# LSH attention and a convolutional feed-forward on one core: weight decoding, convolution taps and the divide with an operand in PSUM

## The chip, the core and the metric

One core of one Trainium2 chip. The metric is device microseconds of one execution, median of the runs shown.

## The reference

Batch 4, 8 heads, 768 positions, head size 64. Keys and queries are hashed to 6 bits each, and a query sees only the keys of its own bucket:

```python
mask = q_bucket[:, :, :, None] == k_bucket[:, :, None, :]
scores = np.where(mask, scale * np.matmul(q, k.transpose(0, 1, 3, 2)), -1000000000.0)
attn = np.exp(scores - np.max(scores, axis=-1, keepdims=True))
attn = attn / (np.sum(attn, axis=-1, keepdims=True) + 1e-09)
x = np.matmul(attn, v)            # then (4, 768, 512), heads side by side
h = np.maximum(x @ w_in, 0.0)     # 512 x 1024
# conv_out: three taps along the sequence, one weight per column and tap
out = h * (1.0 / (1.0 + np.exp(-conv_out))) @ w_out   # 1024 x 512
```

The weights of the feed-forward arrive as float64 and are read as pairs of 32-bit words.

## The kernel before

The order of every engine's instructions is the order of the code. Four batches follow each other, and each has four pairs of heads and then a feed-forward.

A **pair** takes six steps, `i` = 0 to 5 in the loop at L495. It works on two blocks of query columns (416 and 352), three steps each. A step computes the scores of two chunks of 128 keys on TensorE (L294, L295) and their exponentials on ScalarE (L297), and for the chunks of the step before the values (L305) and the row sums' additions: chunks 1 to 4 on GpSimd (L320), chunk 5 on VectorE (L318). The block's last step in line sums over the partitions on TensorE (L328), and VectorE inverts and divides (L331 to L350); the result is split into a high and a low part (L353, L357). Between them the next pair is prepared: row maxima, twelve times two matmuls and a reduction on VectorE (`peak`, L246, L249), in the places that the table `PEAKS` names; the maxima's way through DRAM into row 96 of the queries (`shift_away`, `shift_back`); and for the pair after that the hash (L174), its bits (L180), the high part `hi` of the load `R` (L188), the low part in `R` itself (L192), and the copies into the tiles of Q and K (`place_a`, `place_b`). All those copies and the loads of `R`, `v` and weights go through SP's queue in code order; `bring` (L477) issues at a pair's start the four copies of `place_b`, then the next load of `R`, which must wait until the copies out of `R` have landed, then `v`.

A **feed-forward** has 16 stages (`ffn`, L407): stage `i` computes 128 hidden columns of half the sequence (12 matmuls, L368), ScalarE takes the ReLU and the middle tap, VectorE the two outer taps (L377) and after the sigmoid the product (L381), and GpSimd the low part. `FLAG` = 3 iterations later the stage's output follows (9 matmuls, L392). The hidden banks are a ring of three.

**Weights.** 16 blocks of 128x512 are decoded in batch 0: loaded (`fetch`), |x| on ScalarE (L90), five operations on VectorE (L92 to L100), a cast on ScalarE (L108), two operations on GpSimd (L110, L112). `background` (L132) moves the blocks under way on by some operations at each call. Ten blocks are begun in the pairs of batch 0, six in its feed-forward.

**PSUM** is used as eight banks: a ring S of three times two banks (scores, maxima, sums, outputs) and a ring M of two (values, hash).

## Time and profile before

| | us |
|---|---|
| runs (median) | 809.56, 811.0, 814.94 (811.0) |
| profiled execution | 809.63 |
| its span | 807.8 |

The page gives the busy time of each engine, then the span in 40 slices with the busy share in tenths. [...] In a timeline, a bracket holds the idle time before an instruction and what ended it. "x4" behind a row is a run of four instructions of the same kind.

### The profile page before, as it was taken

What the parts mean: (1) busy time and instruction counts of PE and PEld (TensorE: products, weight loads), DVE (VectorE), ACT (ScalarE), POOL (GpSimd) and SP (SyncE); (2) the same over time, 40 slices, a digit from 0 to 9 for tenths busy, and PEclk for the clock granted to TensorE, in tenths of its full rate; (3) what the DMA queues carried; (4) which work ended last, traced back from release to release, by engine and by line L of the source; (5) the groups of instructions that cost most, each with busy time, mean ns of one, the idle gap of its engine ahead of it and who ended that gap; (6) DMA issues with size and microseconds to landing.
All of it is one profiled execution on the core that took longest, in us unless ns stands there. A gap on an engine that the chain in (4) does not pass through costs nothing.

```text
span 807.8 us, 10032 instructions
## 1 busy us (share of the span) xinstructions
PE 724.2 (90%) x3552; PEld 512.4 (63%) x3552; DVE 562.9 (70%) x758; ACT 361.8 (45%) x582; POOL 404.9 (50%) x264
## 2 busy tenths in 40 slices
PE   6788777786679999999999999999999999999997
PEld 3444443444568855655889755655899755657896
DVE  4479898989895476776766476767766467756664
ACT  4334343435445534444555444444554443445553
POOL 5466666654462374766222365675222466562222
PEclk9797999789789999999999999999999999999999
DMA  4557665625001117646601116655501136500011
GB/s 124 135 179 162 210 174 176 160 47 147 1 0 40 41 24 172 137 113 159 174 4 40 41 37 161 139 148 146 151 0 40 41 69 152 131 3 1 1 40 39
DMA packets 38358, 75.88 MB, mean 94 GB/s; under 512 B 8312, under 2 KB 16774, under 8 KB 38308
## 3 DMA queue, kind: packets, MB, share of 16 engines
q1 hardware_dynamic: 33940, 74.60, 35.1%
q10 hardware_dynamic: 4368, 0.64, 0.5%
q8 instruction: 28, 0.46, 0.2%
q14 instruction: 22, 0.18, 0.1%
HBM read 29.71 MB, written 9.73 MB: 49 GB/s over the span
## 4 chain that ended last, share of the span: by engine, by line
PE 50%; DVE 23%; DMA 15%; issue 5%; ACT 4%; SPq 2%; POOL 1%; ACTq 0%; DVEq 0%
PE o L393 13%; PE v L305 10%; PE spot L368 8%; DMA k<-R 6%; DVE stat L249 5%; PE s L294 5%; DVE ht L377 4%; PE m L246 4%; PE s L295 4%; DMA R<-in_qk 4%; PE h L368 4%; DMA far<-bits 2%; PE sum L328 1%; SPq L207 1%; DVE wuo L92 1%
## 5 line engine op out<-in xcount | busy, mean ns | idle before, releaser
L297 ACT ACTIVATE p<-s 128x836 f32<-128x836 f32 (+1 forms) x192 | 152.8, 810 | 204.9 <-PE s L295 175.9
L249 DVE TENSOR_REDUCE stat<-m 128x1 f32<-128x772 f32 x192 | 181.0, 951 | 80.2 <-PE m L246 79.6
L320 POOL TENSOR_TENSOR ps<-ps,p 128x832 f32<-128x832 f32 (+1 forms) x92 | 161.2, 1752 | 24.2 <-ACT p L297 20.5
L385 POOL TENSOR_TENSOR g<-ht,g 128x384 fp32r<-128x384 f32 x64 | 68.9, 1077 | 207.8 <-ACT g L384 183.7
L305 PE MATMUL v<-p,v 128*64 128x418 f32 (+1 forms) x768 | 155.2, 527 | 13.9 <-DVE bits L180 13.9
L294 PE MATMUL s<-q,k 97*128 97x418 f32 (+1 forms) x384 | 141.1, 368 | 19.5 <-DVE stat L249 9.5
L377 DVE SCALAR_TENSOR_TENSOR ht<-ht,cw 128x384 f32<-128x384 f32 (+1 forms) x128 | 119.1, 931 | 52.3 <-ACT ht L375 49.9
L393 PE MATMUL o<-wo,g 128*128 128x512 f32 x576 | 144.8, 398 | 6.2 <-DVE r L338 6.2
L295 PE MATMUL s<-q,k 128*128 128x418 f32 (+1 forms) x384 | 132.6, 345 | 0.0
L393 PEld LDWEIGHTS o<-wo,g 128*128 128x128 f32 x576 | 108.6, 190 | 28.0 <-DVE r L338 6.6
L246 PE MATMUL m<-k,q 96*128 96x386 f32 x384 | 114.6, 384 | 12.9 <-DVE stat L249 5.9
L320 POOL TENSOR_TENSOR ps<-p,p 128x832 f32<-128x832 f32 (+1 forms) x32 | 60.6, 1893 | 104.9 <-ACT p L297 104.9
L246 PEld LDWEIGHTS m<-k,q 96*128 96x128 f32 x384 | 66.2, 199 | 71.9 <-DVE stat L249 28.6
L294 PEld LDWEIGHTS s<-q,k 97*128 97x128 f32 x384 | 74.2, 193 | 55.3 <-DVE stat L249 20.8
L368 PE MATMUL spot<-xh,wi 128*128 128x386 f32 x320 | 92.5, 351 | 11.7 <-ACT ht L373 11.7
L305 PEld LDWEIGHTS v<-p,v 128*64 128x64 f32 x768 | 48.7, 142 | 77.8 <-issue 60.8
L380 ACT ACTIVATE ht<-ht 128x384 f32<-128x384 f32 x64 | 33.6, 525 | 106.5 <-DVE ht L377 106.5
L295 PEld LDWEIGHTS s<-q,k 128*128 128x128 f32 x384 | 74.7, 194 | 0.7
L368 PEld LDWEIGHTS spot<-xh,wi 128*128 128x128 f32 x320 | 61.0, 194 | 17.3 <-ACT ht L373 13.9
L192 POOL TENSOR_TENSOR R<-R,hi 128x768 fp32r<-128x768 f32 x30 | 59.1, 1971 | 21.6 <-PE hash L174 13.8
L381 DVE TENSOR_TENSOR ht<-ht 128x384 f32<-128x384 f32 x64 | 36.0, 563 | 31.9 <-ACT ht L380 31.9
L368 PE MATMUL spot<-xl,wi 128*128 128x386 f32 x160 | 55.5, 347 | 0.0
(84 smaller groups left out, 735.6 us busy)
## 6 DMA issues: line engine op xcount, KB each, us to landing
R<-in_qk SPq DMA_DIRECT2D x15, 768.0 KB
v<-in_v SPq DMA_DIRECT2D x16, 384.0 KB
k<-hi SPq DMA_DIRECT2D x16, 384.0 KB
q<-hi SPq DMA_DIRECT2D x16, 384.0 KB
out<-osb SPq DMA_DIRECT2D x24, 256.0 KB
q<-R SPq DMA_DIRECT2D x15, 384.0 KB
k<-R SPq DMA_DIRECT2D x15, 384.0 KB
rawi<-in_w_in SPq DMA_DIRECT2D x8, 512.0 KB
```

What stands on the lines that cost most here:

```text
L192: nc.gpsimd.tensor_tensor(R, R.bitcast(F32), self.hi[:, h].bitcast(F32), ALU.subtract)
L246: nc.tensor.matmul(mp[:, half], self.QA[:96, h, t * P:(t + 1) * P], self.K[0][:96, h, half * HS:(half + 1) * HS + 2], start=True, stop=True)
L249: nc.vector.tensor_reduce(self.stat[:, c:c + 1], mp, mybir.AxisListType.XY, ALU.max)
L294: nc.tensor.matmul(sp[:, h], pr.KA[:97, h, ks], pr.Q[0][:97, h, qs], start=True, stop=False)
L295: nc.tensor.matmul(sp[:, h], pr.KB[:, h, ks], pr.Q[1][:, h, qs], start=False, stop=True)
L297: nc.scalar.activation(self.pts[c], sp, AF.Exp, scale=SCALE)
L305: nc.tensor.matmul(self.av[h * D:(h + 1) * D], pr.v[:, c, h, :], self.pts[c][:, h], start=(c == 0), stop=(c == NCK - 1), tile_position=(0, ...
L320: eng.tensor_tensor(self.acc, first if c == 1 else self.acc, pt, ALU.add)
L368: nc.tensor.matmul(hp[:, :HW], w, x[:, c0:c0 + HW], start=(n == 0), stop=(n == 3 * NCC - 1))
L377: nc.vector.scalar_tensor_tensor(t[:, a:z], ht[:, o + k - 1 + a:o + k - 1 + z], cw[:, f, k:k + 1], t[:, a:z], ALU.mult, ALU.add)
L385: nc.gpsimd.tensor_tensor(g[:, 1, :], t, g[:, 0, :].bitcast(F32), ALU.subtract)
L393: nc.tensor.matmul(op, l, r, start=(f == 0 and n == 0), stop=(f == NFC - 1 and n == 2))
```

## The change

Line numbers in the order pieces after the change are those of the changed file: decoding is L106 to L116 there, the reduction of maxima L261, the divide L368, its low part L375, `place_b` L218 and L219, taps L395, product L399.

- Decoding keeps its intermediate in a spare bank of M, so |x| is written to PSUM and each of the five VectorE operations has at most one operand in SBUF. Blocks are begun at steps 2 and 5 of each pair of batch 0 (eight in all) and at iterations 2 to 9 of its feed-forward (eight).
- ReLU works in place in PSUM, and the taps and the product read the hidden stage there. The banks of the hidden ring are the two of S2 (named M2, M3 during a feed-forward) and one of M. The output of a stage follows 4 iterations later in batch 0.
- The divide writes in place in PSUM.
- In batch 0 (`direct`) chunk 5 is not added; `sums` runs over it separately, with two calls more, and 1e-9 is added to the sums.
- `place_b` is in two parts: the copies out of `R` come first, then the load of the next `R` and `v`, then the copies out of `hi`. The hash takes a tile of ring S. The last maximum of a pair moves into the next pair's step 0, `shift_away(4, 2)` from step 0 to 1 and `shift_back(4, 2)` from 1 to 2. Two weight blocks are fetched before the first pair, and two at every third step.

```diff
 FLAG = 3
-RATE = 4
-PEAKS = ((), (1, 2), (0, 1, 2), (0, 1, 2), (1, 2), (1, 2))
-PEAKS_0 = ((0, 1, 2), (0, 1, 2), (0, 1, 2), (0, 1, 2), (1, 2), (1, 2))
+FLAG_0 = 4
+DECODE = 2
+PEAKS = ((2,), (0, 1, 2), (1, 2), (0, 1, 2), (1, 2), (1,))
+PEAKS_0 = ((0, 1, 2), (0, 1, 2), (0, 1, 2), (0, 1, 2), (1, 2), (1,))
...
+    rooms = []
+    def room(name):
+        if rooms:
+            rooms.pop()[0].__exit__(None, None, None)
+        if name:
+            c = tc.tile_pool(name=name, bufs=1, space=PSUM, reuse_waits="tile")
+            rooms.append((c, c.__enter__()))
+    def two_banks(name, k=None):
+        if k is None:
+            k = turns["S"] = (turns.get("S", -1) + 1) % 3
+        pool = rooms[0][1] if k == 2 else ps
+        return pool.tile([P, 2, 512], F32, tag=f"S{k}", name=name, bufs=1)
+    def one_bank(name, k):
+        return (ps if k < 2 else rooms[0][1]).tile([P, 512], F32, tag=f"M{k}", name=name, bufs=1)
...
+    def decode(raw, n, name, bank):
...
+        up, low = (ring(wp, 3, [P, WC], I32, f"w{x}", f"w{x}{name}")[:, :n] for x in "ul")
+        tmp = bank[:, :n]
+        tmpi = tmp.bitcast(I32)
...
-        nc.scalar.activation(lowf, hi, AF.Abs)
-        yield 2
-        V.scalar_tensor_tensor(upf, lowf, F64_MIN, hi, ALU.is_ge, ALU.mult)
-        yield 1
-        V.tensor_scalar(low, up, 3, 0x3FFFFFFF, ALU.logical_shift_left, ALU.bitwise_and)
-        yield 0
-        V.scalar_tensor_tensor(up, up, -0x40000000, low, ALU.bitwise_and, ALU.bitwise_or)
-        yield 2
-        V.tensor_scalar(low, up, -0x800000, None, ALU.bitwise_and)
-        yield 0
-        V.scalar_tensor_tensor(lowf, lo, 2.0 ** -52, lowf, ALU.mult, ALU.mult)
+        nc.scalar.activation(tmp, hi, AF.Abs)
+        yield
+        V.scalar_tensor_tensor(upf, tmp, F64_MIN, hi, ALU.is_ge, ALU.mult)
+        yield
+        V.tensor_scalar(tmpi, up, 3, 0x3FFFFFFF, ALU.logical_shift_left, ALU.bitwise_and)
+        yield
+        V.scalar_tensor_tensor(up, up, -0x40000000, tmpi, ALU.bitwise_and, ALU.bitwise_or)
+        yield
+        V.tensor_scalar(tmpi, up, -0x800000, None, ALU.bitwise_and)
+        yield
+        V.scalar_tensor_tensor(lowf, lo, 2.0 ** -52, tmp, ALU.mult, ALU.mult)
...
+    def split_weight(raw, name, bank):
+        up, low = yield from decode(raw, WC, name, bank)
+        yield
+        yield
         blk = weights[name] = cp.tile([P, 2, WC], F32R, tag=f"w{name}", name=f"w{name}")
         nc.scalar.copy(blk[:, 0, :], up)
-        yield 2
+        yield
         nc.gpsimd.tensor_tensor(up, up, blk[:, 0, :].bitcast(F32), ALU.subtract)
-        yield 1
         nc.gpsimd.tensor_tensor(blk[:, 1, :], up, low, ALU.add)
 
...
+    def spare_bank(name):
+        return one_bank(name, (turns.get("M", 1) + 1) % 2)
+    def decode_next():
+        raw, name = fetched.pop(0)
+        decoding[0] = split_weight(raw, name, spare_bank(f"d{name}"))
+    def decode_on(n=1):
+        for _ in range(n):
+            next(decoding[0], None)
 
...
-            hp = ring(ps, 2, [P, 512], F32, "M", f"hash{self.nm}")
-            turns["M"] -= 1
+            hp = two_banks(f"hash{self.nm}")[:, 0, :]
...
-        def place_b(self):
-            hi, lo = self.hi.bitcast(F32), self.R.bitcast(F32)
-            QB, KB = self.QB.bitcast(F32), self.KB.bitcast(F32)
-            for dst, src in ((QB[:64], hi[:64]), (KB[64:], hi[64:]), (QB[64:], lo[:64]), (KB[:64], lo[64:])):
-                nc.sync.dma_start(dst, src)
+        def place_b(self, low):
+            src = (self.R if low else self.hi).bitcast(F32)
+            QB, KB = (t.bitcast(F32)[64 * k:64 * k + 64] for t, k in ((self.QB, low), (self.KB, 1 - low)))
+            nc.sync.dma_start(KB, src[64:])
+            nc.sync.dma_start(QB, src[:64])
...
+            self.direct = pair.b == 0
...
         def add(self, c):
 
-            if c == 0:
+            if c == 0 or (self.direct and c == NCK - 1):
                 return
             if c == 1:
                 self.acc = ring(wp, EB, [P, 2, WMAX], F32, "e", f"ps{self.nm}")[:, :, :self.w]
-            last = self.j == 1 and self.pair.p == NP - 1
+            last = self.j == 1 and self.pair.p == NP - 1 and not self.direct
             eng = nc.vector if c > DADD - last else nc.gpsimd
...
             self.sm = bank[:, :w]
-            for h in range(2):
-                nc.tensor.matmul(self.sm[h * D:(h + 1) * D], ones, self.acc[:, h],
-                                 start=True, stop=True, tile_position=(0, h * D))
+            parts = [self.acc] + [self.pts[-1][:, :, self.n - w:]] * self.direct
+            for k, part in enumerate(parts):
+                for h in range(2):
+                    nc.tensor.matmul(self.sm[h * D:(h + 1) * D], ones, part[:, h], start=(k == 0),
+                                     stop=(k == len(parts) - 1), tile_position=(0, h * D))
...
             nc.vector.transpose(self.tt[:, 0, :w], self.sm)
-            nc.vector.reciprocal(rec, self.tt[:, 0, :w].rearrange("p (j r) -> p j r", r=32)[:, :, 0])
+            total = self.tt[:, 0, :w].rearrange("p (j r) -> p j r", r=32)[:, :, 0]
+            if self.direct:
+                nc.vector.tensor_scalar(rec, total, 1e-9, None, ALU.add)
+                total = rec
+            nc.vector.reciprocal(rec, total)
             self.rec = rec
...
-            self.xf = self.tt[:, 0, :w]
-            nc.vector.scalar_tensor_tensor(self.xf, self.av[:, self.n - w:], pr.mean, self.tt[:, 1, :w],
-                                           ALU.add, ALU.mult)
+            self.xf = self.av[:, self.n - w:]
+            nc.vector.scalar_tensor_tensor(self.xf, self.xf, pr.mean, self.tt[:, 1, :w], ALU.add, ALU.mult)
...
-        ht = ring(wp, EB, [P, 2, WMAX], F32, "e", f"ht{b}_{half}_{f}").rearrange("p a b -> p (a b)")
-        t = ht[:, 388:388 + HS]
-        nc.scalar.activation(ht[:, :HW], hp[:, :HW], AF.Relu)
+        hp = hp[:, :HW]
+        t = ring(wp, EB, [P, 2, WMAX], F32, "e", f"ht{b}_{half}_{f}")[:, 0, :HS]
         o = 0 if half == 0 else HW - HS
-        nc.scalar.activation(t, ht[:, o:o + HS], AF.Copy, scale=cw[:, f, 1:2])
+        nc.scalar.activation(hp, hp, AF.Relu)
+        nc.scalar.activation(t, hp[:, o:o + HS], AF.Copy, scale=cw[:, f, 1:2])
         for k, a, z in ((0, half == 0, HS), (2, 0, HS - (half == 1))):
-            nc.vector.scalar_tensor_tensor(t[:, a:z], ht[:, o + k - 1 + a:o + k - 1 + z], cw[:, f, k:k + 1],
+            nc.vector.scalar_tensor_tensor(t[:, a:z], hp[:, o + k - 1 + a:o + k - 1 + z], cw[:, f, k:k + 1],
                                            t[:, a:z], ALU.mult, ALU.add)
         yield None
         nc.scalar.activation(t, t, AF.Sigmoid)
-        nc.vector.tensor_tensor(t, ht[:, o:o + HS], t, ALU.mult)
+        nc.vector.tensor_tensor(t, hp[:, o:o + HS], t, ALU.mult)
...
-        s0, m0 = turns["S"], (turns["M"] + 1) % 2
-        spot = ps.tile([P, 2, 512], F32, tag=f"S{(s0 + 1) % 3}", name=f"spot{b}", bufs=1)
+        m0, flag = turns["M"], FLAG if b else FLAG_0
+        room(f"ffn{b}")
 
         def bank(i):
-            k = i % 2 if i < 4 else (i - 1) % 3
-            if k == 0:
-                return ps.tile([P, 512], F32, tag=f"M{m0}", name=f"h{b}_{i}", bufs=1)
-            return spot[:, k - 1, :]
-        for i in range(len(todo) + FLAG):
-            fill(i, ps.tile([P, 2, 512], F32, tag=f"S{s0}", name=f"spare{b}", bufs=1) if i == 2 else None)
+            return one_bank(f"h{b}_{i}", 2 + i % 2 if i < 4 else (2, 3, m0)[(i - 4) % 3])
...
+            decode_on(3)
+            if i >= DECODE and fetched:
+                decode_next()
+                decode_on(3)
...
             if i == len(todo) + 1:
-                turns["S"] = s0
+                room(f"heads{b + 1}")
+                turns["S"] = 1
...
+                half, f = todo[i - flag]
                 if f == 0:
-                    acc[half] = [ps.tile([P, 2, 512], F32, tag=f"S{(s0 + 3 - k) % 3}", name=f"o{b}_{half}_{k}",
-                                         bufs=1) for k in range(2)]
-                output(b, half, f, gs[i - FLAG], acc[half])
+                    acc[half] = [two_banks(f"o{b}_{half}_{k}", 1 - k) for k in range(2)]
...
+            if i >= DECODE:
+                decode_on(3)
...
-    splits.append(decode_taps(cwr))
+    fetch(2)
...
         if n < len(pairs):
-            pairs[n].place_b()
+            pairs[n].place_b(1)
         if n + 1 < len(pairs):
             pairs[n + 1].load()
         if n < len(pairs):
             pairs[n].load_v()
+            pairs[n].place_b(0)
...
-            if i == 1 and n:
+            if i == 2 and n:
                 pr.shift_back(4, 2)
...
-                    if i == 0 and n:
+                    if i == 1 and n:
                         pr.shift_away(4, 2)
...
+                    decode_on()
...
+            if pr.b == 0 and i % 3 == 2:
+                if n == 0 and i == 2:
+                    decoding[0] = decode_taps(cwr, spare_bank("dcw"))
+                    decode_on(6)
+                decode_next()
+            decode_on()
...
-            background(RATE, 1)
+            decode_on()
...
-            if n or i:
-                fetch(1)
-            background(RATE, 1)
+            if i % 3 == 0:
+                fetch(2 if n else 1)
+            decode_on(4 if i == 5 and pr.p == NP - 1 else 1)
```

VectorE, from the end of pair 1 of batch 0 into pair 2, before (`stat` holds row maxima, `wui`, `wli` and `rawi` a block of weights, `ps` row sums):

```order
L249 TENSOR_REDUCE stat_83<-m_2_5_1_739 128x1
L268 STREAM_TRANSPOSE side_2_4_743<-stat_83 128x32
L92 SCALAR_TENSOR_TENSOR wui_1_754<-wli_1_755,rawi_1_466 128x512
L318 SCALAR_TENSOR_TENSOR ps_1_1_683<-ps_1_1_683,p_1_1_5_724 128x2x352
L94 TENSOR_SCALAR wli_1_755<-wui_1_754 128x512
L96 SCALAR_TENSOR_TENSOR wui_1_754<-wui_1_754,wli_1_755 128x512
L249 TENSOR_REDUCE stat_84<-m_3_0_0_813 128x1
```

The same place after it (`di` is the bank of PSUM, `xl` the low part of a pair's result):

```order
L261 TENSOR_REDUCE stat_83<-m_2_5_0_729 128x1
L375 TENSOR_TENSOR xl_1_710<-v_1_0_549,xh_1_709 128x416
L108 SCALAR_TENSOR_TENSOR wui_0_735<-di_0_734,rawi_0_385 128x512
L110 TENSOR_SCALAR di_0_734<-wui_0_735 128x512
L112 SCALAR_TENSOR_TENSOR wui_0_735<-wui_0_735,di_0_734 128x512
L114 TENSOR_SCALAR di_0_734<-wui_0_735 128x512
L116 SCALAR_TENSOR_TENSOR wli_0_736<-rawi_0_385,di_0_734 128x512
L261 TENSOR_REDUCE stat_83<-m_2_5_1_785 128x1
```

The addition of chunk 5 is gone from the row, and the five operations on a block stand together between two reductions.

SP's queue at the start of pair 1 of batch 0, before:

```order
L207 DMA q_0_76<-hi_2_368 64x2x768
L207 DMA k_0_80<-hi_2_368 64x2x768
L207 DMA q_0_76<-R_2_210 64x2x768
L207 DMA k_0_80<-R_2_210 64x2x768
L161 DMA R_3_481<-in_qk 128x2x768
L165 DMA v_2_483<-in_v 128x768
L128 DMA rawi_1_509<-in_w_in 128x1024
```

The same place after it:

```order
L218 DMA k_0_80<-R_2_215 64x2x768
L219 DMA q_0_76<-R_2_215 64x2x768
L174 DMA R_3_483<-in_qk 128x2x768
L178 DMA v_2_485<-in_v 128x768
L218 DMA k_0_80<-hi_2_382 64x2x768
L219 DMA q_0_76<-hi_2_382 64x2x768
L144 DMA rawi_1_517<-in_w_in 128x1024
```

The copies out of `R` moved ahead of those out of `hi`, and the loads of the next `R` and of `v` stand between the two.

VectorE in the feed-forward of batch 0, after the change (stage 2, and the first block begun there; before it L92 to L96 and L98, L100 stood behind the products of two stages):

```order
L395 SCALAR_TENSOR_TENSOR ht_0_2_1397<-h_2_1384,cw,ht_0_2_1397 128x383
L395 SCALAR_TENSOR_TENSOR ht_0_2_1397<-h_2_1384,cw,ht_0_2_1397 128x384
L108 SCALAR_TENSOR_TENSOR wuo_1405<-do_1404,rawo_791 128x512
L110 TENSOR_SCALAR do_1404<-wuo_1405 128x512
L399 TENSOR_TENSOR ht_0_2_1397<-h_2_1384,ht_0_2_1397 128x384
L112 SCALAR_TENSOR_TENSOR wuo_1405<-wuo_1405,do_1404 128x512
L114 TENSOR_SCALAR do_1404<-wuo_1405 128x512
L116 SCALAR_TENSOR_TENSOR wlo_1406<-rawo_791,do_1404 128x512
```

A whole block stands in one iteration, around the stage's product.

## Rows read from the trace of the kernel before

**Rows 1.** The page of the profile: the busy time of each engine (its section 1), and one line of its section 2, VectorE's busy share in tenths, where the span of 807.8 us stands in 40 slices of 20.2 us.

```profile
PE 724.2 (90%) x3552; PEld 512.4 (63%) x3552; DVE 562.9 (70%) x758; ACT 361.8 (45%) x582; POOL 404.9 (50%) x264
...
DVE  4479898989895476776766476767766467756664
```

**Rows 2.** Busy time of each engine in four stretches (us from the span's start, length, then busy us and number of instructions by engine, granted clock, DMA share, GB/s). In order: three pairs of batch 0, one pair of batch 2, the feed-forward of batch 0 and that of batch 2, each from its first hidden matmul to the end of its last output matmul.

```profile
53.50:172.90 119.40, 92.78 (x410) 52.06 (x408) 109.04 (x131) 44.81 (x66) 79.11 (x47) 0.87 0.60 161
477.60:504.80 27.20, 26.23 (x142) 15.92 (x140) 18.48 (x30) 11.96 (x16) 16.79 (x11) 1.00 0.60 146
182.10:278.30 96.20, 77.60 (x353) 67.73 (x354) 75.02 (x94) 46.05 (x86) 39.42 (x30) 0.89 0.14 39
563.80:634.90 71.10, 70.93 (x353) 62.21 (x353) 44.70 (x61) 37.27 (x72) 16.87 (x16) 1.00 0.22 58
```

**Rows 3.** The timeline (start us, duration us, engine, line, operation): VectorE's mean of the first block of pair 0 and of pair 3 in batch 0 and of the last pair of batch 2, and the first hidden matmul of the feed-forward of batches 0 and 2 on TensorE.

```profile
53.52 0.14 DVE L335 TENSOR_SCALAR mean<-v 128x1 f32<-128x1 f32 x1
...
172.89 0.14 DVE L335 TENSOR_SCALAR mean<-v 128x1 f32<-128x1 f32 x1
...
558.54 0.15 DVE L335 TENSOR_SCALAR mean<-v 128x1 f32<-128x1 f32 x1
...
182.15 0.45 PE L368 MATMUL h<-xh,wi 128*128 128x386 f32 x1 [0.50 <-DVE r L349]
...
563.82 0.34 PE L368 MATMUL h<-xh,wi 128*128 128x386 f32 x1
```

**Rows 4.** The timeline of VectorE at the start of pair 2 of batch 0: the last addition of a block's row sums and the two operations on a block of weights behind it, and the same two operations on the next block.

```profile
106.85 1.97 DVE L318 SCALAR_TENSOR_TENSOR ps<-ps,p 128x704 f32<-128x704 f32 x1
108.75 2.21 DVE L94 TENSOR_SCALAR wli<-wui 128x512 int32<-128x512 int32 x1
110.98 2.20 DVE L96 SCALAR_TENSOR_TENSOR wui<-wui,wli 128x512 int32<-128x512 int32 x1
...
122.84 0.41 DVE L94 TENSOR_SCALAR wli<-wui 128x512 int32<-128x512 int32 x1
123.28 0.69 DVE L96 SCALAR_TENSOR_TENSOR wui<-wui,wli 128x512 int32<-128x512 int32 x1
```

**Rows 5.** The timeline of GpSimd over the same microseconds.

```profile
110.84 4.01 POOL L320 TENSOR_TENSOR ps<-ps,p 128x832 f32<-128x832 f32 x2 [0.18 <-ACT p L297]
```

**Rows 6.** Groups of instructions by line and form (count, then busy us in all and mean ns of one, then idle time before them and what ended it).

```profile
L180 DVE TENSOR_SCALAR bits<-hash,cst 128x384 fp32r<-128x384 f32 x15 | 9.1, 610 | 5.8 <-PE hash L174 5.8
...
L90 ACT ACTIVATE wli<-rawi 128x512 f32<-128x512 f32 x8 | 5.3, 668 | 0.0
...
L110 POOL TENSOR_TENSOR wui<-wui,wi 128x512 f32<-128x512 f32 x8 | 10.2, 1278 | 23.9 <-ACT wi L108 23.9
```

**Rows 7.** Line 377, the convolution taps, and line 318, the last addition of a block's row sums: count, then duration in ns (least, median, most).

```profile
L377 DVE SCALAR_TENSOR_TENSOR ht<-ht,cw x128: 604/622/1540, 189.2 to 796.6; 128x383 f32<-128x383 f32 x64, 128x384 f32<-128x384 f32 x64
...
L318 DVE SCALAR_TENSOR_TENSOR ps<-ps,p x32: 848/983/2468, 49.7 to 734.0; 128x832 f32<-128x832 f32 x16, 128x704 f32<-128x704 f32 x16
```

**Rows 8.** The chain of waits that ended last, in order of time (start us, us, what): the sums of one block in a pair of batch 2; an output and a hidden stage in a later feed-forward.

```profile
478.29 0.70 PE sum L328 x4
...
432.01 2.08 PE o L393 x9
...
434.09 2.12 PE spot L368 x12
```

**Rows 9.** The timeline of TensorE and VectorE in the feed-forward of batch 2: the first matmul of hidden stage 3, the product that ends stage 1, and the taps of stage 2.

```profile
572.65 0.34 PE L368 MATMUL spot<-xh,wi 128*128 128x386 f32 x1
...
573.46 0.56 DVE L381 TENSOR_TENSOR ht<-ht 128x384 f32<-128x384 f32 x1 [0.59 <-ACT ht L380]
...
575.85 1.27 DVE L377 SCALAR_TENSOR_TENSOR ht<-ht,cw 128x383 f32<-128x383 f32 x2
```

**Rows 10.** What TensorE waited for from 34 to 187 us, the pairs of batch 0 (us in total, times, longest us).

```profile
PE s L294 <- DVE stat L249: 9.3, 6, 2.8
PE v L305 <- DVE bits L180: 7.5, 4, 2.0
PE s L294 <- ACT p L297: 6.6, 3, 3.0
PE m L246 <- DVE stat L249: 5.9, 4, 1.8
```

**Rows 11.** The same over the whole span, two kinds.

```profile
PE v L305 <- DVE bits L180: 13.9, 8, 2.0
...
PE hash L174 <- DMA R<-in_qk: 6.9, 6, 1.6
```

**Rows 12.** A pair of batch 2 in the chain of waits (start us, us, what): the last copy out of R until it landed, and the load of the next R; and from the timeline the cast of that R on ScalarE (start us, us; in brackets the idle time before it).

```profile
489.83 6.88 DMA k<-R
...
496.76 4.33 DMA R<-in_qk
...
501.16 1.57 ACT L188 CAST hi<-R 128x768 fp32r<-128x768 f32 x2 [2.50 <-DMA R<-in_qk]
```

**Rows 13.** The way of a pair's row maxima: in the chain of waits of batch 3 the copy to DRAM until it landed (start us, us), and in the timeline of ScalarE's queue in batch 2 the issue of the copy to DRAM and that of the copy back behind it.

```profile
680.27 4.81 DMA top<-side
...
484.57 0.55 ACTq L273 DMA_DIRECT2D top<-side  x1
...
486.64 0.58 ACTq L276 DMA_DIRECT2D q<-top  x1
```

More of the change, by code (lines that the diff above doesn't have):

```diff
@@ L39 @@
 DADD = 4
-HRATE = 2.5
 WC = 512
@@ L75, in lsh_attention_conv_ffn @@
     nc.vector.memset(ones, 1.0)
-    def decode(raw, n, name):
+    def decode(raw, n, name, bank):
         pr = raw.rearrange("p (n two) -> p n two", two=2)
         lo, hi = pr[:, :, 0].bitcast(U32), pr[:, :, 1].bitcast(F32)
-        up, low = (ring(wp, bufs, [P, WC], I32, f"w{x}", f"w{x}{name}")[:, :n]
-                   for x, bufs in (("u", 3), ("l", 3)))
+        up, low = (ring(wp, 3, [P, WC], I32, f"w{x}", f"w{x}{name}")[:, :n] for x in "ul")
+        tmp = bank[:, :n]
+        tmpi = tmp.bitcast(I32)
@@ L110, in split_weight, with decode_taps @@
         nc.gpsimd.tensor_tensor(up, up, blk[:, 0, :].bitcast(F32), ALU.subtract)
-        yield 1
         nc.gpsimd.tensor_tensor(blk[:, 1, :], up, low, ALU.add)
-    def decode_taps(raw):
-        up, low = yield from decode(raw, NFC * 3, "cw")
+    def decode_taps(raw, bank):
+        up, low = yield from decode(raw, NFC * 3, "cw", bank)
         nc.vector.tensor_tensor(cw.rearrange("p f k -> p (f k)"), up, low, ALU.add)
@@ L121, in lsh_attention_conv_ffn @@
     blocks += [(w_out[f * P:(f + 1) * P], f"o{f}") for f in range(NFC)]
-    fetched, splits, step = [], [], [0]
+    fetched, decoding = [], [iter(())]
     def fetch(n):
@@ L130, in fetch @@
         del blocks[:n]
-    def background(rate, stop):
-        step[0] += 1
-        if rate and len(fetched) > (2 if blocks else 0) and step[0] // rate > (step[0] - 1) // rate:
-            splits.append(split_weight(*fetched.pop(0)))
-        now = splits[:]
-        while now:
-            for g in now[:]:
-                ended = next(g, None)
-                if ended is None:
-                    splits.remove(g)
-                if ended is None or ended >= stop:
-                    now.remove(g)
+    def spare_bank(name):
[6 more added lines that the diff above has]
+            next(decoding[0], None)
     class Pair:
@@ L254, in shift_now @@
         def shift_now(self, t0, n):
-            tp = ring(ps, 3, [P, 2, 512], F32, "S", f"mt{self.nm}_{t0}")
+            tp = two_banks(f"mt{self.nm}_{t0}")
             for h in range(2):
@@ L324, in sums @@
             if bank is None:
-                bank = ring(ps, 3, [P, 2, 512], F32, "S", f"sum{self.nm}")[:, 0, :]
+                bank = two_banks(f"sum{self.nm}")[:, 0, :]
             self.sm = bank[:, :w]
-            for h in range(2):
-                nc.tensor.matmul(self.sm[h * D:(h + 1) * D], ones, self.acc[:, h],
-                                 start=True, stop=True, tile_position=(0, h * D))
+            parts = [self.acc] + [self.pts[-1][:, :, self.n - w:]] * self.direct
[3 more added lines that the diff above has]
+                                     stop=(k == len(parts) - 1), tile_position=(0, h * D))
         def invert(self):
@@ L586, in lsh_attention_conv_ffn @@
             ffn(pr.b, [pairs[pr.b * NP + c].x for c in range(NCC)], fill, ahead)
+    room(None)
 def kernel(q, k, v, proj, moe_w_in, moe_conv_w, moe_w_out):
```

17 lines of the change are left out of this document (7 added, 10 removed).

## The prediction

> **What bounds the kernel now.** I read the busy times of the page first. TensorE is busy for 724.2 of 807.8 us, but the line of VectorE's slices starts with six slices of 8 or 9 behind the first, and later stands at 6 or 7 [rows 1]. So batch 0 has another limit than the rest, and I read stages apart [rows 2]. A pair of batch 2 takes 27.20 us, of which TensorE works 26.23 at full clock. Three pairs of batch 0 take 119.40, 39.8 each, with TensorE at 92.78 and VectorE at 109.04, 91%. The feed-forward of batch 2 is TensorE alone (70.93 of 71.10); that of batch 0 takes 96.20, with neither engine full (77.60 and 75.02). Batch 0 thus costs 3 x 12.6 + 25.1 = 63 us above the pace of batch 2, and its weights are the reason. That is the pool from which the change can take.
>
> The third view is the timeline of VectorE beside GpSimd's. The two operations on a block of weights at 108.75 and 110.98 take 2.21 and 2.20 us; on the next block the same two take 0.41 and 0.69 [rows 4]. The addition of chunk 5 ahead of them has 1.97, where its median is 0.983 and its least 0.848, its most 2.468 [rows 7]. Over the same microseconds GpSimd adds with 2.0 each [rows 5]. So each engine's operations on SBUF are drawn out by the other's, and much of the 91% is not work. Last, the waits: TensorE in the pairs of batch 0 waits for VectorE's maxima, its bits, and exponentials [rows 10].
>
> How the executions stand: the profiled one took 809.63 us, 1.83 outside its span of 807.8; the median is 811.0. The sum is made against 809.63. About 1% is what a measurement of this kernel can tell from no change.
>
> **The pairs of batch 0.** VectorE's work in a pair without weights is 18.48 us [rows 2]. The addition of chunk 5 goes twice (0.98 + 0.85 by [rows 7]): 16.65. Two blocks of five operations come. No row shows one of them with its operand in PSUM. The nearest are the bits, which read PSUM (384 elements, 610 ns [rows 6]), against the taps from SBUF (383 or 384 elements, least 604 [rows 7]): the place costs 0.01 us. Clean, a decoding operation has 0.69 with two operands and 0.41 with one [rows 4]; I take 0.69 for all five, minus 0.07 by which a start overlaps the end before it (108.75 against 106.85 + 1.97 [rows 4]): 0.62, so 10 x 0.62 = 6.2. The new addition of 1e-9 is as small as the mean, 0.14 [rows 3], twice 0.3. Each block's first operation may wait for the |x| of ScalarE, 0.67 [rows 6]: 1.3. VectorE then needs 16.65 + 6.2 + 0.3 + 1.3 = 24.5 us. TensorE needs 27.2 and the second pass of the sums, 0.70 a block [rows 8]: 28.6. So TensorE becomes the bound, and a pair can't be shorter than 28.6. Above, all waits of [rows 10] but that for bits could stay: (9.3 + 5.9 + 6.6)/4 = 5.4, so 34.0. I take 30.0, near the lower end, because VectorE has 4 us free. Three pairs: -3 x 9.8 = **-29.4**. In pair 0 I count only the wait for bits, 7.5/4 [rows 10]: **-1.9**. From the mean of pair 3 to the first hidden matmul it takes 9.26 us in batch 0 and 5.28 in batch 2 [rows 3]; of these 4.0 I take **-3.0**, since the decoding there stays.
>
> [...]
>
> **The feed-forward of batch 0.** All eight w_out blocks are decoded here, one in each of the iterations 2 to 9. The taps of stage 2 start 575.85 - 563.82 = 12.0 us after the first hidden matmul [rows 3, 9]. An iteration of VectorE has two taps of 0.62 [rows 7], five decodings of 0.69, a product of 0.56 [rows 9], less eight overlaps: 4.7. Eight: 37.6. The last block's cast (as the |x|, 0.67) and two operations on GpSimd (1.28 [rows 6]): 3.2. Then nine outputs and four hidden stages of 2.1 [rows 8]: 27.3. In all 80.1 against 96.2: **-16.1**. Below, with the two single-operand decodings at 0.41, 75.6; above, with a stretch in each iteration as the taps now show it (1.54 - 0.60 [rows 7]), 87.6. TensorE and GpSimd have room under it: VectorE sets the pace for the eight iterations.
>
> **The feed-forwards 1 to 3.** A hidden bank now stays in use until the product. Hidden stage 3 must wait for the product of stage 1; before, it began at 572.65, and that product ended at 573.46 + 0.56 [rows 9]. The difference of 1.4 shrinks by some 0.6 (two taps not drawn out); 0.8 in each: **+2.4**. Between 0 and 1.4 each, 0 to 4.2.
>
> **The order of the copies.** The last copies out of R land 6.88 us after 489.83, and the next R takes 4.33 [rows 12]. With two of the four copies ahead of the load it starts half of 6.88, 3.4, sooner. What hash waits for R (6.9) and the rest of the wait for bits (13.9 - 7.5 = 6.4 [rows 10, 11]) can go: -13.3. Against it: the copies out of hi now stand behind R and v on SP's queue, and end at 489.83 + 3.4 + 4.3 + 2.2 (v has half of R's bytes) + 3.4 = 503.2; the next hi is cast at 501.16 [rows 12]. The cast would be 2.0 late. It stands ahead of exponentials on ScalarE and of the next early copies; for 11 pairs +22. The maxima of step 4 also wait for the bits, since hash takes a turn of ring S. I take **0**, because R's earlier landing and hi's later one offset each other, and keep both ends. The fetch ahead of the first pair (1 MB) moves on a queue that has nothing else: 0. The divide in PSUM: VectorE's work is the same, 0; its bank of M is held through the low part, and the next values start in the other: 0.
>
> **Sum.** -29.4 - 1.9 - 3.0 - 16.1 + 2.4 = -48.0, and 809.63 - 48.0 = 762.
>
> **Rivals.**
> - *The engines keep alternating in batch 0.* A pair stays at 34.0, as its waits on maxima and exponentials do not come from drawn-out operations: 762 + 12 = 774. For it speaks that 9.3 of the wait is for maxima [rows 10]; against it that VectorE falls from 36 to 25 us a pair. 0.12.
> - *The small additions are locked out.* The addition of 1e-9 has source and target in SBUF, and TENSOR_SCALAR of that kind is the one that went from 0.41 to 2.21 [rows 4]. Eight blocks by 1.8 on the path: 776. Against it: it does little, and VectorE has room. 0.06. [...]
> - *The copies out of hi are late*, as worked out: 784. Against it: ScalarE is busy for 45% only [rows 1]. 0.10.
> - *The waits in later batches vanish*: 762 - 13 = 749. 0.06.
> - *Something else holds batch 0's pairs*, so that the change does there nothing of what it says: the DMA share is 0.60 at 39.8 us, and would be 0.80 at 30. Only the feed-forwards gain: 809.63 - 16.1 + 2.4 = 796. 0.04, half of it within 1%.
> - *Slower: the maxima of the last two query tiles.* They leave for DRAM a step later. The way took 4.81 in one pair of the chain [rows 13]. If the second block's scores wait that long in each of 15 pairs: 762 + 72 = 834. It decides from 48.0/15 = 3.2 us a pair. Against it: the copy back was issued 2.1 us behind the copy out [rows 13], and two steps of 27.20/6 = 4.5 are left. 0.04.
>
> **How the numbers follow.** The forecast has 0.58: 762. The range from 746 to 788 holds it with its bounds (pairs at 28.6 give 4 less, the feed-forward -4.5 to +7.5), the alternating engines, the small additions, late copies and the gain in later batches; outside are the last two, and tails. Faster by over 1%: 0.94; within 1%: 0.02; slower: 0.04.
>
> **What would show it.** Right: pairs of batch 0 near 30 us with VectorE at 25 and its decodings near 0.6 to 0.7, no operation of 2 us among them; the feed-forward of batch 0 near 80; batches 1 to 3 within 5 us of before; hash without a wait for R, and hidden stage 3 with a wait for the product of stage 1. Wrong: decodings still above 1 us; pairs of batch 0 above 35; a cast of hi that waits for copies; a wait of scores for q from `top` in step 3.

## The result

The changed kernel takes 787.7 us (median of 781.8, 787.5, 788.0, 791.8), the kernel before 812.1 in the same runs: ratio 0.9693, 95% interval [0.9622, 0.9764]. That is 24 us faster, half of the 48 forecast. The forecast of 762 was 25.7 too low, and the time lies at the very edge of the range of 746 to 788. The profiled execution took 781.79 us (span 780.0), so it stands at the fast end of its runs. Times, here and below, are medians of all executions; the ratios leave out five executions that lie over 1.5% above the fastest of their kernel, among them one of 1115 us in experiment 4.

The page after, against [rows 1]. Behind the first three slices VectorE had nine in a row at 8 or 9; now the pairs of batch 0 stand at 7, and 8, 9 and 8 remain in its feed-forward (a slice is 19.5 us here):

```profile
PE 716.5 (92%) x3584; PEld 505.0 (65%) x3584; DVE 481.6 (62%) x757; ACT 358.8 (46%) x582; POOL 392.3 (50%) x265
...
DVE  5387777789844676666444666576453666746443
```

The windows after: three pairs of batch 0, three of batch 2, the feed-forwards of batch 0 and batch 2 ([rows 2] have one pair of batch 2). The granted clock, behind the busy times, is TensorE's; 1.00 is full speed:

```profile
52.00:148.20 96.20, 83.56 (x435) 48.69 (x433) 75.82 (x115) 42.97 (x61) 67.33 (x43) 1.00 0.71 183
443.20:526.10 82.90, 79.28 (x413) 47.62 (x411) 55.01 (x85) 35.15 (x48) 50.83 (x30) 0.99 0.59 143
155.30:240.40 85.10, 75.63 (x357) 63.40 (x358) 61.58 (x103) 46.83 (x89) 44.11 (x37) 0.98 0.19 50
531.50:603.30 71.80, 71.23 (x354) 62.47 (x355) 34.38 (x59) 36.19 (x72) 16.26 (x16) 1.00 0.22 59
```

The limits of the stages of batch 0 in the timelines, as in [rows 3]:

```profile
51.99 0.15 DVE L350 TENSOR_SCALAR mean<-v 128x1 f32<-128x1 f32 x1
...
148.25 0.15 DVE L350 TENSOR_SCALAR mean<-v 128x1 f32<-128x1 f32 x1
...
155.34 0.44 PE L386 MATMUL h<-xh,wi 128*128 128x386 f32 x1 [0.45 <-ACT p L310]
```

By these limits in the two traces, the difference of 27.8 us in span is made up as follows (0.3 lies behind the last output):

| term | forecast | traces |
|---|---|---|
| three pairs of batch 0 (119.4 to 96.3) | -29.4 | -23.1 |
| pair 0, tail of pair 3 | -1.9, -3.0 | -1.5, -2.2 |
| feed-forward of batch 0 (96.3 to 85.0) | -16.1 | -11.3 |
| feed-forwards 1 to 3 | +2.4 | +1.4 |
| pairs of batches 1 to 3, their gaps and tails | 0 | +9.2 |

What TensorE waited for after, the whole span, names two new waits, for `top` and for `bits` ahead of maxima, in place of those of [rows 11]:

```profile
PE m L258 <- DVE bits L192: 9.0, 10, 1.9
PE m L258 <- DVE stat L261: 7.8, 8, 1.6
PE s L307 <- DMA q<-top: 7.6, 8, 2.0
PE o L411 <- POOL wo L128: 6.4, 7, 2.2
```

The theory from this trace: the maxima's later way costs in batches 1 to 3, and in batch 0 the small additions and the real pace of decoding. The rivals: the hash's place, and the copies out of `hi`, for which ScalarE's casts wait now:

```profile
ACT hi L200 <- DMA q<-hi: 20.3, 8, 3.7
```

### The profile page after: what moved, and what is told of

Same layout as the page of the kernel before. It is cut to its first block, busy times and chain, and to the rows that moved or that the text cites. A ratio compares the mean times of both kernels' runs of the same rounds, so it can differ in the third digit from the quotient of the medians.

```text
span 780.0 us, 10064 instructions
## 1 busy us (share of the span) xinstructions
PE 716.5 (92%) x3584; PEld 505.0 (65%) x3584; DVE 481.6 (62%) x757; ACT 358.8 (46%) x582; POOL 392.3 (50%) x265
## 4 chain that ended last, share of the span: by engine, by line
PE 63%; DVE 16%; DMA 11%; issue 4%; ACT 3%; POOL 2%; SPq 1%; DVEq 0%; POOLq 0%; ACTq 0%
PE o L411 17%; PE h L386 15%; PE v L318 12%; PE m L258 7%; DVE stat L261 6%; PE s L307 5%; PE s L308 4%; DMA q<-top 3%; DMA top<-side 3%; PE sum L343 3%; DMA q<-hi 2%; DMA rawi<-in_w_in 1%; DVE rec L356 1%; DVE bits L192 1%; DVE ht L395 1%
## 5 line engine op out<-in xcount | busy, mean ns | idle before, releaser
L261 DVE TENSOR_REDUCE stat<-m 128x1 f32<-128x772 f32 x192 | 180.9, 949 | 95.6 <-PE m L258 95.4
L403 POOL TENSOR_TENSOR g<-ht,g 128x384 fp32r<-128x384 f32 x64 | 65.1, 1018 | 187.0 <-ACT g L402 176.4
L386 PE MATMUL h<-xh,wi 128*128 128x386 f32 x512 | 144.1, 342 | 6.5 <-DVE ht L399 4.4
L318 PE MATMUL v<-p,v 128*64 128x418 f32 (+1 forms) x768 | 149.9, 512 | 0.0
L307 PE MATMUL s<-q,k 97*128 97x418 f32 (+1 forms) x384 | 137.7, 359 | 12.8 <-DMA q<-top 7.6
L395 DVE SCALAR_TENSOR_TENSOR ht<-h,cw,ht 128x384 f32<-128x384 f32 (+1 forms) x128 | 78.9, 616 | 79.9 <-ACT ht L393 77.6
L258 PEld LDWEIGHTS m<-k,q 96*128 96x128 f32 x384 | 63.5, 195 | 88.4 <-issue 32.9
L386 PEld LDWEIGHTS h<-xh,wi 128*128 128x128 f32 x512 | 94.2, 188 | 17.5 <-DVE ht L399 7.2
L333 POOL TENSOR_TENSOR ps<-p,p 128x832 f32<-128x832 f32 (+1 forms) x32 | 58.7, 1833 | 77.4 <-ACT p L310 77.4
L386 PE MATMUL h<-xl,wi 128*128 128x386 f32 x256 | 86.8, 339 | 0.0
L392 ACT ACTIVATE h<-h 128x386 f32<-128x386 f32 x64 | 30.5, 477 | 57.5 <-PE h L386 57.2
```

Source lines behind the costliest of these rows:

```text
L258: nc.tensor.matmul(mp[:, half], self.QA[:96, h, t * P:(t + 1) * P], self.K[0][:96, h, half * HS:(half + 1) * HS + 2], start=True, stop=True)
L261: nc.vector.tensor_reduce(self.stat[:, c:c + 1], mp, mybir.AxisListType.XY, ALU.max)
L307: nc.tensor.matmul(sp[:, h], pr.KA[:97, h, ks], pr.Q[0][:97, h, qs], start=True, stop=False)
L318: nc.tensor.matmul(self.av[h * D:(h + 1) * D], pr.v[:, c, h, :], self.pts[c][:, h], start=(c == 0), stop=(c == NCK - 1), tile_position=(0, ...
L333: eng.tensor_tensor(self.acc, first if c == 1 else self.acc, pt, ALU.add)
L386: nc.tensor.matmul(hp[:, :HW], w, x[:, c0:c0 + HW], start=(n == 0), stop=(n == 3 * NCC - 1))
```

## The experiments

Ratios are to the kernel before on the same chip, with their 95% interval. "Less" and "more" are differences of ratios times 811 us. Lengths of stages come from one profiled execution of each version. Three versions whose code for the pairs of batch 0 is the same (experiments 6, 10 and the second run of 4) have 31.2, 31.5 and 30.7 us a pair there, so a difference of under 1 us a pair shows nothing.

**1. The small addition left out.**

```diff
-                nc.vector.tensor_scalar(rec, total, 1e-9, None, ALU.add)
-                total = rec
```

> The changed kernel without the addition of 1e-9 to the row sums of batch 0 (left out of the computation there). After the change those eight operations on 13 or 11 elements take 173 to 1611 ns, median 1103. If they are locked out by GpSimd and lie on the path (the rival of the prediction), the three pairs of batch 0 take 30 to 31 us each instead of 32.1, and the time falls by 4 to 8 us. If VectorE has room for them, the pairs stay within 0.4 us of 32.1 and the time within 1.5 us.

783.3 us, 0.9666 [0.9626, 0.9706]: 2 us less than the changed kernel, inside the interval. The pairs of batch 0 went to 31.3 us each, but the waits for `top` rose from 7.6 to 14.2 in that execution. Inconclusive alone.

**2. The maxima as before** (`PEAKS_0` likewise; the comments are added here).

```diff
-PEAKS = ((2,), (0, 1, 2), (1, 2), (0, 1, 2), (1, 2), (1,))
+PEAKS = ((), (1, 2), (0, 1, 2), (0, 1, 2), (1, 2), (1, 2))
-            if i == 2 and n:      # shift_back
+            if i == 1 and n:
-                    if i == 1 and n:      # shift_away
+                    if i == 0 and n:
```

> The changed kernel with the places of the row maxima, and the steps at which the maxima of the last two query tiles leave and come back, as before the change. The pairs of batches 1 to 3 cost 9.2 us more after the change (gaps, pairs and tails together), and TensorE waits 7.6 us for q from top. If the later way of the maxima is what costs, those waits go and the time falls by 5 to 9 us. If it is not, the time stays within 2 us.

774.1 us, 0.9545 [0.9502, 0.9589]: 12 us less. The three pairs of batch 2 take 79.9 us:

```profile
440.50:520.40 79.90, 78.28 (x411) 47.14 (x409) 55.44 (x85) 34.89 (x48) 49.43 (x29) 1.00 0.60 148
```

They took 82.9 in the changed kernel and 80.9 before (by [rows 2, 3]). Batches 1 to 3 without their feed-forwards take 308.5 us here, 320.5 in the changed kernel and 311.3 before: the 12 us lie there, and the rest of the change makes these batches 2.8 us shorter. ScalarE's casts wait for the copies out of `hi` for 29.9 us in this run, more than the 20.3 of the changed kernel, so those waits are not the 12 us.

**3. The late steps alone**: the places of the maxima as before (the `PEAKS` lines of experiment 2), the two steps as changed.

> The changed kernel with the old places of the row maxima, but with the way of the last two query tiles at the later steps of the change (away in step 1, back in step 2). If the step at which they leave and come back is what costs, the time is that of the changed kernel, 783 to 789 us, and scores wait for q from top again. If only the place of the last maximum costs, it is 770 to 776.

786.1 us, 0.97 [0.9636, 0.9763], the time of the changed kernel. The steps are the cause, not the place. Its trace shows how, in batch 1. First SP's queue, then the chain, then ScalarE and its queue, then the windows of one stretch:

```profile
272.10 0.60 SPq L218 DMA_DIRECT2D k<-R  x1
272.75 0.60 SPq L219 DMA_DIRECT2D q<-R  x1
278.75 0.39 SPq L174 DMA_DIRECT2D R<-in_qk  x1
```

```profile
273.05 5.82 DMA top<-side
```

```profile
273.05 0.54 ACTq L285 DMA_DIRECT2D top<-side  x1
...
278.89 0.59 ACTq L288 DMA_DIRECT2D q<-top  x1
279.59 0.87 ACT L310 ACTIVATE p<-s 128x836 f32<-128x836 f32 x1 [4.97 <-PE s L308]
```

```profile
273.00:279.00 6.00, 5.88 (x30) 3.54 (x28) 3.69 (x7) 1.62 (x2) 4.23 (x3) 1.00 0.62 138
279.00:284.00 5.00, 3.48 (x10) 1.07 (x10) 2.16 (x3) 1.98 (x3) 1.80 (x1) 0.70 0.84 254
281.10:284.10 3.00, 3.00 (x10) 0.78 (x9) 1.39 (x2) 0.48 (x1) 1.30 (x1) 0.50 1.01 366
```

and TensorE's values of one step ahead of the stall and of one behind it, with the maxima's matmuls between:

```profile
273.94 1.62 PE L318 MATMUL v<-p,v 128*64 128x418 f32 x8
...
280.51 0.67 PE L258 MATMUL m<-k,q 96*128 96x386 f32 x2 [1.60 <-ACT p L310]
281.11 3.06 PE L318 MATMUL v<-p,v 128*64 128x418 f32 x8
```

The 16 KB of `top` are issued 0.3 us behind the second of two copies of 384 KB out of R and land when these do: 278.87, and the next R, which waits for them, is issued at 278.75. The copy back is issued in order on ScalarE's queue, so the exponentials behind it wait too: the bracket blames the scores, but the last release is the issue at 278.89. Then TensorE stands idle for 1.60 us, and from 281.1 to 284.1 its granted clock is 0.50: the eight matmuls of the values take 3.06 us where they took 1.62 at 1.00. So this place loses time twice, but that the idle time brings the slower matmuls is not shown. Two waits for `top` in the changed kernel, of 1.95 and 1.99 us, have a clock of 1.00 in the 4 us behind them, and eight values there take 1.62 again; one of 1.93 us, for `bits`, has 0.63:

```profile
336.29 0.40 PE L307 MATMUL s<-q,k 97*128 97x352 f32 x1 [1.95 <-DMA q<-top]
...
338.65 1.62 PE L318 MATMUL v<-p,v 128*64 128x418 f32 x8
```

```profile
336.29:340.29 4.00, 4.00 (x21) 2.48 (x21) 1.92 (x2) 1.52 (x2) 1.17 (x1) 1.00 0.96 230
671.70:675.70 4.00, 4.00 (x21) 2.48 (x21) 1.92 (x2) 1.52 (x2) 1.18 (x1) 1.00 0.00 0
259.60:263.60 4.00, 4.00 (x14) 1.37 (x14) 1.03 (x2) 0.00 (x0) 3.92 (x3) 0.63 0.38 82
```

With the early steps (experiment 2) `top` leaves before the copies, and 2.1 us suffice:

```profile
447.16 0.54 ACTq L285 DMA_DIRECT2D top<-side  x1
...
449.30 0.58 ACTq L288 DMA_DIRECT2D q<-top  x1
```

```profile
449.11 0.61 SPq L218 DMA_DIRECT2D k<-R  x1
```

It is not one place alone. In batches 1 to 3 there are eight steps at which such copies out of `R` go out near `top`. From the issue of `top` to that of the copy back it takes 2.1 to 2.3 us in all eight in experiment 2, 3.4 to 5.8 here, and 3.0 to 5.1 in the changed kernel; here the copy back follows the second copy out of `R` by 5.1 to 6.1 us every time.

**4. The hash in ring M** (from the third pair of batch 1 on; the condition on the pair is left out here).

```diff
-            hp = two_banks(f"hash{self.nm}")[:, 0, :]
+            hp = ring(ps, 2, [P, 512], F32, "M", f"hash{self.nm}")
+            turns["M"] -= 1
```

> The changed kernel with the hash of the pairs of batches 1 to 3 (from the third pair of batch 1 on) in a bank of ring M as before the change, in place of a tile of ring S. If the turn of ring S costs, the wait of the maxima for bits (9.0 us, 10 times) goes and the time falls by 4 to 9 us. If the wait only moves back to the values (13.9 us before), the time stays within 2 us or grows by up to 4.

791.1 us, 0.974 [0.97, 0.978]: 4 us more than the changed kernel, and the intervals overlap. Repeated without the late maxima, on the version of experiment 6:

> The run of 767.1 us with the hash of batches 1 to 3 in a bank of ring M as before the change. If the turn of ring S costs the 9.0 us that maxima wait for bits, the time falls by 4 to 9. If the wait moves to the values, as in the kernel before (13.9 us), the time grows by 1 to 5.

767.3 us, 0.9442 [0.939, 0.9494], the same as 767.1. The wait of the maxima goes and 4.8 us of wait of the values come; no effect of the place on the time shows.

**5. The copies in the old order.**

```diff
+            pairs[n].place_b(0)
             pairs[n].place_b(1)
...
             pairs[n].load_v()
-            pairs[n].place_b(0)
```

> The changed kernel with all four copies of place_b ahead of the next load of R, as before the change. If the late copies out of hi are what costs in batches 1 to 3, the time falls by 4 to 9 us. If the sooner load of R is a gain (hash waited 6.9 us for it before), hash waits for R again and the time grows by 3 to 7 us.

798.2 us, 0.9853 [0.9814, 0.9893]: 13 us more. With the late maxima this has two readings, so it was repeated on the version of experiment 6:

> The run of 767.1 us (old places of the maxima, small addition to PSUM) with all four copies of place_b ahead of the load of R again. If the order of the copies is a gain of its own (hash waited 6.9 us for R before the change), the time grows by 4 to 12 us and hash or the maxima wait for R or the bits. If it cost only because the copies stood ahead of the late maxima in the DMA engines, the time stays within 2 us.

771.7 us, 0.9462 [0.9373, 0.9551], against 0.9455 for that version: the time shows no difference. The traces say more. With the late maxima, the copy back is issued 5.0 to 5.5 us behind `top` in all eight places, against 3.0 to 5.1 with two copies ahead of it, so behind four copies a late `top` took longer still; but the maxima also wait 19.3 us for bits instead of 9.0. With the early maxima, hash waits 2.7 us for `R` again, and the pairs of batches 1 and 2 take 8.1 us more than in experiment 6, while those of batch 0 take 3.3 less. So by the times most of the 13 us hang on the late maxima; whether R's sooner load is a gain of its own, of up to 8 us by this one trace, stays open.

**6. The small addition to PSUM**, with the maxima as before.

```diff
-            self.sm = bank[:, :w]
+            self.sm, self.total = bank[:, :w], bank[:, 480:480 + w // 32]
...
-                nc.vector.tensor_scalar(rec, total, 1e-9, None, ALU.add)
-                total = rec
+                nc.vector.tensor_scalar(self.total, total, 1e-9, None, ALU.add)
+                total = self.total
```

> The changed kernel with the old places and steps of the maxima (as the run before this, 774.1 us), and the addition of 1e-9 in batch 0 written to PSUM in place of SBUF. Without that addition the first pairs lost 2.3 us, pair 0 and the tail 0.6 each. If its cost is a lockout of an operation from SBUF to SBUF, the eight additions fall from 1.1 us to under 0.3, and the time by 2 to 4 us, to 770 to 772. If it waits for something else, it keeps 1 us or more, and the time stays.

`bank` is the bank of the sums in PSUM. 767.1 us, 0.9455 [0.9404, 0.9506]: 7 us less than experiment 2, with intervals that just touch, where 2 to 4 were expected; the spans of the two traces differ by 5.1. It is the fastest version, 5.4% under the kernel before. Line 356 in the changed kernel (least, median, most ns), and here:

```profile
L356 DVE TENSOR_SCALAR rec<-r x8: 173/1103/1611, 54.5 to 165.5; 128x13 f32<-128x13 f32 x4, 128x11 f32<-128x11 f32 x4
```

```profile
L356 DVE TENSOR_SCALAR sum<-r x7: 180/183/185, 53.8 to 147.9; 128x13 f32<-128x13 f32 x4, 128x11 f32<-128x11 f32 x3
```

The eighth addition here writes a tile of another name and takes 0.18 too. Only the target of the addition moved, and with it the source of the reciprocal behind it, and 1.1 us became 0.18. The pairs of batch 0 went from 32.6 to 31.2 us, 4.3 of the 5.1. What the addition waited for stands in the trace of the changed kernel, on VectorE and GpSimd:

```profile
118.58 1.54 DVE L356 TENSOR_SCALAR rec<-r 128x13 f32<-128x13 f32 x1
...
165.51 0.17 DVE L356 TENSOR_SCALAR rec<-r 128x11 f32<-128x11 f32 x1
```

```profile
118.39 1.69 POOL L333 TENSOR_TENSOR ps<-p,p 128x704 f32<-128x704 f32 x1
...
163.06 1.01 POOL L403 TENSOR_TENSOR g<-ht,g 128x384 fp32r<-128x384 f32 x1
166.69 1.01 POOL L403 TENSOR_TENSOR g<-ht,g 128x384 fp32r<-128x384 f32 x1 [2.62 <-ACT g L402]
```

The addition that began at 118.58 ended at 120.12, just behind GpSimd's addition (120.08); the one at 165.51 met an idle GpSimd and took 0.17. Each of the seven long ones ends 0.02 to 0.04 us behind the end of the GpSimd operation beside it, so I read their length as a wait for that operation.

**7. Each operand back in SBUF**, with the maxima as before (774.1).

The intermediate of decoding (`tmp, tmpi = lowf, low`):

> The changed kernel with the old places of the maxima (774.1 us), and the intermediate of decoding back in SBUF; order of the instructions the same. By the prediction the place is what frees the decoding: operations over 2 us come back, the pairs of batch 0 go from 32.6 to 36 to 40 us, and the time grows by 10 to 25 us. If the gain in batch 0 came from the new order and the missing addition of chunk 5 alone, the time grows by less than 4.

789.0 us, 0.9711 [0.9649, 0.9773]: 13 us more, within the 10 to 25 expected, but not where it was expected. The pairs stay (96.5 us for three, 97.9 with PSUM); the feed-forward of batch 0 goes from 86.4 to 100.9. The groups of one operation with two operands on the blocks decoded in the pairs, with the intermediate in SBUF (this run) and in PSUM (experiment 2; count, sum, mean ns):

```profile
L111 DVE SCALAR_TENSOR_TENSOR wui<-wui,wli 128x512 int32<-128x512 int32 x8 | 12.5, 1565 | 0.1
```

```profile
L112 DVE SCALAR_TENSOR_TENSOR wui<-wui,di 128x512 int32<-128x512 int32 x8 | 5.5, 682 | 0.1
```

The stretch is real in the pairs (1565 against 682 ns), and hidden there beside TensorE: VectorE's busy time in the three pairs rises from 75.5 to 85.3 us, in a stretch of 96 to 98 of which TensorE works 84 to 87.

ReLU, taps and product (`activation(ht[:, :HW], hp[:, :HW], AF.Relu)`, then `hp = ht`):

> The changed kernel with the old places of the maxima (774.1 us), and ReLU, taps and product of a hidden stage back in SBUF (the banks stay as changed). By the prediction the taps in batch 0 are drawn out again beside GpSimd (up to 1.54 against 0.60) while the wait of hidden stage 3 goes: its feed-forward from 86.4 to 90 to 94 us, the others 0.5 us less each, the time 2 to 6 us more. If the taps in PSUM buy nothing, the time falls by 1 to 2.

790.1 us, 0.9737 [0.9672, 0.9801]: 16 us more, where 2 to 6 were expected. The feed-forward of batch 0 takes 93.5, 7.0 more, the tail of pair 3 takes 2.7 more, and the other feed-forwards 0.5 to 0.8 less; this is as expected. The pairs of batches 1 and 2 take 11.8 us more, which was not expected. One `top` there takes 5.47 us in the chain; it is issued at 280.59, between the two copies out of `R` (280.00 and 280.64). That is one place of eight, and where the rest of the 11.8 comes from stays open.

Chunk 5 on VectorE (`self.direct = False`):

> The changed kernel with the old places of the maxima (774.1 us), and chunk 5 in batch 0 added on VectorE again as before the change (without the second pass of the sums on TensorE and the small addition). If VectorE's load sets the pairs of batch 0, the two additions of 0.85 to 2.5 us cost more than the 2 x 0.70 of TensorE and the small additions: 3 to 10 us more. If the swap was even, the time stays within 2 us.

778.4 us, 0.959 [0.9537, 0.9643]: 4 us more, with overlapping intervals; the three pairs take 2.0 us more, which equal code can show too, and the feed-forward 2.8.

**8. Order alone**: all operands in SBUF and chunk 5 added.

> The changed kernel with the old places of the maxima (774.1 us) and all operands as before the change: the intermediate of decoding, ReLU, taps, product and divide in SBUF, chunk 5 added on VectorE. What stays of the change is the order of decoding, its spread (eight and eight blocks), the earlier fetch, the copies and the banks. If the operands in PSUM bring the gain in the pairs of batch 0 together, though the intermediate alone brought nothing there, the pairs go back from 32.6 to 36 to 40 us and the time is 800 to 815. If the spread and order bring it, the pairs stay at 32 to 34 and the time is 790 to 800.

800.4 us, 0.9866 [0.983, 0.9903]. The pairs take 34.8 us each (39.8 before the change, 32.6 in experiment 2), the feed-forward of batch 0 108.3, 12 more than before the change. In the pairs the operands (and chunk 5) bring 2.2 of 7.2 us; in the feed-forward they bring all, 22, against 12 that two more blocks and their order cost.

**9. The spread alone**, in the kernel before (`RATE = 6`, `HRATE = 1.5`).

> The kernel before with one edit: decoding is begun at every sixth call in the pairs in place of the fourth (two blocks a pair in place of three), and faster in the feed-forward, which then takes nine of the sixteen blocks in place of six. Operands and all else as before. If the spread brought the pairs of batch 0 from 39.8 to 34.8, they take 34 to 36 us here, and the feed-forward of batch 0 grows from 96 to 108 to 115; the time is 805 to 815. If the order and the earlier fetch brought it, the pairs stay above 38.

818.1 us, ratio 1.0073 [1.0039, 1.0106], 6 us more than the kernel before. The pairs take 38.1 us each, so the spread is 1.7 of the 5.0; the feed-forward of batch 0 takes 112.5. The copies do not hold the rest: with them in the old order the pairs of batch 0 take 32.0 against 32.1 and 30.1 against 31.2 us (the two runs of experiment 5). It lies in the order of the five operations, the banks and the earlier fetch, which were not parted.

**10. Decoding from iteration 0** (`DECODE = 0`, and `decode_on(3 + (i == 0))`), on the version of experiment 6.

> The run of 767.1 us (old places of the maxima, small addition to PSUM) with the first w_out block begun at iteration 0 of the feed-forward of batch 0 in place of 2. If VectorE's chain of eight iterations of 5.2 us sets that feed-forward's length, it starts sooner where VectorE had idle time: 86.0 us become 78 to 82, and the time falls by 4 to 8. If another engine holds the stage (GpSimd's two operations on a block, for which the outputs wait 6.9 us), it stays within 2 us.

767.7 us, 0.9458 [0.94, 0.9516]: the same. The feed-forward went from 86.0 to 84.0; outputs no longer wait for weights (6.9), but hidden stages wait 7.9 for products. In the eight iterations of the changed kernel VectorE is busy for 39.96 of 41.66 us:

```profile
167.06:208.72 41.66, 33.01 (x149) 27.36 (x148) 39.96 (x67) 24.36 (x48) 26.77 (x23) 0.96 0.16 45
```

Here it is busy for 41.93 of 43.85 us in its eight. So VectorE's queue is the limit while blocks are decoded. That an earlier start brings nothing because the products then wait in this queue fits the waits, but no further run tested it.

## Why the prediction was wrong

- **Pairs of batch 0.** The term was 6.3 us too large, and that it came so near is luck in part. TensorE did become the limit: 83.56 of 96.20 us busy, clock 1.00. The duration of a decoding operation holds (0.68 to 0.70 us, for 0.69). Two steps failed. The small additions stood in the sum at 0.3 us a pair, and their being drawn out beside GpSimd only as a rival of 0.06: seven of the eight took 0.52 to 1.61 us, at about half the price that the rival gave (7 of 14 us), and with PSUM as target they took 0.18 and the pairs come to 31.2. And the mechanism, that the intermediate in PSUM frees the pairs, is not what made them shorter: experiment 7 shows no effect there beyond the 1 us a pair that equal code can show, and by experiment 8 some 5.0 of 7.2 us a pair come with all operands in SBUF, from order, spread, fetch and banks, which the term did not count.
- **Feed-forward of batch 0.** The term was mis-sized by 4.8. An iteration takes 5.2 us, not 4.7, as this stretch shows from taps to taps:

```profile
177.51 1.26 DVE L395 SCALAR_TENSOR_TENSOR ht<-h,cw,ht 128x383 f32<-128x383 f32 x2
178.82 0.69 DVE L108 SCALAR_TENSOR_TENSOR wuo<-do,rawo 128x512 f32<-128x512 f32 x1
179.55 0.69 DVE L110 TENSOR_SCALAR do<-wuo 128x512 int32<-128x512 int32 x1
180.15 0.55 DVE L399 TENSOR_TENSOR ht<-h,ht 128x384 f32<-128x384 f32 x1
180.62 0.68 DVE L112 SCALAR_TENSOR_TENSOR wuo<-wuo,do 128x512 int32<-128x512 int32 x1
181.33 0.70 DVE L114 TENSOR_SCALAR do<-wuo 128x512 int32<-128x512 int32 x1
182.06 0.69 DVE L116 SCALAR_TENSOR_TENSOR wlo<-rawo,do 128x512 f32<-128x512 uint32 x1
182.67 1.26 DVE L395 SCALAR_TENSOR_TENSOR ht<-h,cw,ht 128x383 f32<-128x383 f32 x2
```

  Where an operation here reads the result of the one before, it starts 0.03 to 0.04 us behind its end (L110, L114, L116); the overlaps, 0.08 to 0.09, stand in this stretch only between independent ones. I had taken the overlap of 0.07 for all. The eight iterations take 41.66 in place of 37.6, which is 4.1 of the 4.8; the outputs and stages at the end take the rest.
- **Feed-forwards 1 to 3.** Right: +0.5 each for 0.8, hidden stages wait for products as forecast, and experiment 7 takes it back.
- **Batches 1 to 3, "I take 0".** This is the step that failed most: the later way of the row maxima stood in the sum at nothing, and the runs showed 12 us for it. The rival on it, at 0.04, had the right place and sign and the wrong size: 72. Its counter-argument, that the copy back follows the copy out by 2.1 us [rows 13] with two steps left, held only for the step at which `top` leaves ahead of the large copies; behind them it was 3.0 to 5.1 us in the changed kernel, and the copy back, issued one step later on ScalarE's queue, held the exponentials behind it. I had the moved copies and the moved maxima in separate terms; together they cost, by `top` landing with copies of 384 KB. The offsets between copies and hash that I did take as 0 came to -2.8, near enough; that the casts of `hi` wait for copies, which I had named as a sign of being wrong, did show, but was not the 12 us (experiment 2).
- Without the two costs found, 12 and 7 us, the kernel takes 767.1, 5 us above the forecast; of the mis-sized terms the pace of decoding stays.
- Two readings of rows were loose, without a part in the error: the line of VectorE's slices has nine at 8 or 9 behind the first three, not six behind the first, and GpSimd's additions of [rows 5] stand beside the second of the two drawn-out operations only (beside the first stands one of 2.66 us from 108.00).
